# Two attentions and a gate on one core: five score products and six maxima tasks issued in another order

## The chip, the core and the metric

The kernel runs on one core of one Trainium2 chip. A core has a matrix engine (PE, whose weight loads the profile lists apart as PEld), a vector engine (DVE), a scalar engine (ACT), a general engine (POOL) and SyncE (SP), which here only starts transfers. Each engine runs its own instructions in the order in which the program issued them; semaphores tie the engines together. Matrix products land in PSUM, eight banks of 512 fp32 columns for each of 128 partitions. The metric is the device time of one execution in microseconds (us), and of several runs the median.

## The reference: what is computed

Input x has 2048 rows of 512 columns; there are 32 heads of 16 columns. Two attention blocks read the same x, and a gate mixes them:

```
g = sigmoid((x * gate_w).sum(-1))
a: q, k, v = x @ wq, x @ wk, x @ wv; 4 segments of 512 rows:
   p = softmax(q k^T / 4 + causal mask), within the segment
   o = sigmoid(beta) * (phi(q) M) / (phi(q) z + 1e-6) + (1 - sigmoid(beta)) * (p v)
   then M += phi(k)^T v, z += sum phi(k);  phi(t) = t + 1 if t > 0 else exp(t)
   a = o @ A_wo
b: q, k, v = x @ wqkv; p = softmax(q k^T / 4) over all 2048 rows; b = (p v) @ B_wo
out = g * a + (1 - g) * b
```

A is causal within a segment of 512 rows and carries a memory from segment to segment; B is full attention over 2048 rows.

## The kernel before, in words

**Units.** The work is cut into 64 units, each of four heads and 512 queries: units 0 to 31 belong to A, units 32 to 63 to B. After a stage of projections (up to about 400 us of the profile), the main loop runs 32 steps. Step k computes unit 32 + k of B and unit k of A, and beside them the row maxima that the softmax of the next units needs.

**Positions.** A step has NG = 37 positions n. At positions 0 to 31 stand the 32 groups of score products of B, and at 32 to 36 the five groups of A (`GA`). A position issues, in this order: `t_group` (the transposed score products of two heads, L537, and two exponentials on ACT, L543, that write the weights to `raw`); the work that `plan` and `extras` hold for the position; and `pvs`, products with the values into the bank `pvb` (L559). In A, POOL then clears the part above the diagonal (L546). The tasks of `plan` at a position of B go inside `t_group`, between its first and its second product (`mid`).

**Maxima tasks.** `s_b` (L467) and `s_a` (L442) make score products again, untransposed, into one of the two double banks `sbk`, and DVE reduces each to its row maxima (L476 for B; L460 or L462 for A). The two double banks are taken in turn, so a task waits until DVE has read the task two before it. Positions 0 to 31 have one `s_b` task each. Positions 32 to 36 have the six `s_a` tasks in the order of `ST_A` (L700): one at 32, one at 33, two at 34, one at 35, one at 36. A task (i, p) of A handles row block i, 128 queries that see 128 * (i + 1) keys: (3, p) has 512 columns in each of two products, (2, p) has 384; (1, None) does both pairs p with 256 columns each, and (0, None) both with 128. Each pair p adds four small mask products (L456). Longer rows cost DVE more.

**Halves of the array.** Scores contract over 64 rows, so a product uses the upper or the lower half of the array (j = 0 or 1), and products of different halves run side by side. Products with the values use all 128 rows.

**The output projection.** From step 9 to step 30, position 1 also holds `out_rows` (L639): 24 products in 12 pairs (upper half, lower half) of the weights `wh`, `wl` with the rows `oh`, `ol` (L644), accumulating in one misc bank and one half of an `sbk`. Steps alternate between a = 0 and a = 1, the two input halves; a = 1 adds up and stores. After its third pair, out_rows issues the tasks handed to it as `inner`: in these steps the one `s_b` task that `plan` holds for position 1. `split` work for the next rows (`oh` on ACT, `ol` on POOL, L622) stands at the end of every even step.

**Banks.** `t_group`, `out_rows` and `m_rows` draw from the three banks T3 = tb0, tb1, mb; `bank` (L88) hands out the one that was taken longest ago. A group that takes a bank waits until ACT has read it.

**The A order elsewhere.** The first six tasks of A (unit 0) are taken in the same order from a list that is issued in pairs inside the projection stage (L764, L783).

Of the kernel before, what the change touches and what calls it, by code (L numbers as in the profile page):

```python
# [23 lines left out]
NT = SEQ // 128  # L24
# [10 lines left out]
def gated_mix_kernel(ctx, tc, xt, wq, wk, wv, wo, beta, wqkv, wob, gate_w, out):  # L35
# [49 lines left out]
    SBK = [PS.tile([128, 2, C], FT, name=f"sbk{i}") for i in range(2)]  # L85
    lru = []

    def bank(allowed):  # L88
        b = min(allowed, key=lambda a: max([n for n, x in enumerate(lru) if x is a], default=-1))
        lru[:] = [x for x in lru if x is not b] + [b]  # L90
        return b
# [3 lines left out]
    def misc():  # L95
        return bank(mode["misc"])
# [12 lines left out]
    def rot(key, lst):  # L109
        i = cnt.get(key, 0)  # L110
        cnt[key] = i + 1
        return lst[i % len(lst)]
# [287 lines left out]
    def q_of(u):  # L400
        return QA[u % 2] if u < 32 else QB[u % 3]

    def k_of(u, p):
        return KA[u % 2][:, p] if u < 32 else KB[(u - 32) % 3][:, p]
# [113 lines left out]
    AT = {}  # L518
# [3 lines left out]
    def t_group(u, n, banks, between=()):  # L522


        kd, qd, c = UN[u]
        bs = [bank(banks) for _ in range(2)]
        c0 = 0
        for it, hs in (((n // 2, (n % 2 * 2, n % 2 * 2 + 1)),) if kd == "B" else GA[n]):
            q0 = 128 * it if kd == "A" else 0
            w = C - q0  # L530
            pn = it if kd == "B" else it % 2
            for j, h in enumerate(hs):
                if j:
                    for f in between:
                        f()
                r = slice(64 * j, 64 * j + 64)
                nc.tensor.matmul(bs[j][:, c0:c0 + w], k_of(u, h // 2)[r, 128 * it:128 * it + 128],  # L537
                                 q_of(u)[r, h // 2, q0:], start=True, stop=True)
                PT[u, it, h] = PTILE[pn % 2][:, 2 + j if (kd, it) == ("A", 2) else h][:, c0:c0 + w]
            c0 += w  # L540
        for j in range(2):
            pt = PTILE[pn % 2][:, 2 + j if (kd, n) == ("A", 4) else hs[j]]
            nc.scalar.activation(pt, bs[j], AF.Exp, scale=SCALE)  # L543
            if kd == "A":
                m = pt[:, :128] if n < 2 else pt.rearrange("p (a t) -> p a t", a=4)[:, ::3 if n < 4 else 2]
                nc.gpsimd.affine_select(out=m, in_=m, pattern=[[1, 128]] if n < 2 else [[0, 2], [1, 128]],  # L546
                                        compare_op=OP.is_ge, fill=0.0, base=0, channel_multiplier=-1)
# [89 lines left out]
            nc.sync.dma_start(outr[tt * 128:(tt + 1) * 128, :], AT["yo"])  # L637

    def out_rows(c, t, a, inner):  # L639
        b = [misc(), rot("s", SBK)[:, 0]]  # L640
        for n, (oi, wi, g) in enumerate([(oi, wi, g) for oi, wi in TERMS for g in range(4)]):
            for j in range(2):
                r = slice(64 * j, 64 * j + 64)
                nc.tensor.matmul(b[j], (AT["oh"], AT["ol"])[oi][r, g, a], (AT["wh"], AT["wl"])[wi][r, g, a],  # L644
                                 start=n == 0, stop=n == 11)
            if n == 2:
                for f in inner:
                    f()
                rot("s", SBK)
        if a == 0:  # L650
            AT["y"] = [AT["L"].tile([128, DM], FT, name=n) for n in ("yo", "yp")]
            nc.scalar.activation(AT["y"][0], b[0], AF.Copy)
            nc.vector.tensor_copy(AT["y"][1], b[1])
        else:
            tt = 4 * c + t
            y0, y1 = AT["y"]
            y2 = AT["L"].tile([128, DM], FT, name="yq")
            nc.scalar.activation(y2, b[0], AF.Copy)
            nc.vector.tensor_tensor(y1, b[1], y1, op=OP.add)
            nc.gpsimd.tensor_tensor(y0, y0, y2, op=OP.add)  # L660
            nc.gpsimd.tensor_tensor(y0, y0, y1, op=OP.add)
            nc.sync.dma_start(outr[tt * 128:(tt + 1) * 128, :], y0)
# [33 lines left out]
    def todo(fn, *a):  # L696
        return lambda: fn(*a)

    ST_B = [(i, p, kc) for i in range(4) for p in range(2) for kc in range(4)]
    ST_A = [(3, 0), (3, 1), (2, 0), (2, 1), (1, None), (0, None)]  # L700

    def s_tasks(u):
        return [todo(s_a, u, *t) for t in ST_A] if u < 32 else [todo(s_b, u, *t) for t in ST_B]

# [83 lines left out]
    for blk in range(16):  # L788
        g, c = divmod(blk, 4)
        pg, pc = divmod(blk - 1, 4)  # L790
        if blk == 4:
            mode["misc"] = TB + [MB, PVB]
        rate = len(ST_A + ST_B) / SPILLS if 4 <= blk < 14 else 0
        if blk == 14:
# [3 lines left out]
        n = blk + 1 + (c == 2)  # L798
# [74 lines left out]
    def late():  # L873
        proj.close()
        L = AT["L"] = ctx.enter_context(tc.tile_pool(name="late", bufs=1))
        VB[1] = L.tile([128, NT, 8, E + 1], FT, name="vb1")
        AT["o"] = [L.tile([128, 4, 2, C], FT, name=f"o{n}") for n in range(2)]
        AT["wh"] = L.tile([128, 4, 2, DM], FR, name="wh")
        AT["wl"] = L.tile([128, 4, 2, DM], FR, name="wl")
        AT["d"] = [L.tile([128, C], FT, name=f"d{n}") for n in range(2)]  # L880
        AT["oh"] = L.tile([128, 4, 2, 128], FR, name="oh")
        AT["ol"] = L.tile([128, 4, 2, 128], FR, name="ol")
        for p in range(2):
            set_aux(KB[2][:, p], 0)

    T3 = TB + [MB]
# [4 lines left out]
    def pvs(k, n):  # L891

        ua, ub = k, 32 + k
        if n == 0:
            if k:
                pv(ua - 1, 2)
                fin_copy(ua - 1)
        elif k == 31 and n < 2 * NT:
            if n % 2 and n > 1:
                pv(ub, n // 2 - 1)  # L900
        elif 2 <= n < 2 * NT + 2:
            pv(ub, n // 2 - 1, n % 2 * 256, n % 2 * 256 + 256)
            if n == 2 * NT + 1:
                fin_copy(ub)
        elif n > 2 * NT + 1:
            m = n - 2 * NT - 2
            if m < 2:
                pv(ua, 0, 256 * m, 256 * m + 256)
            else:
                pv(ua, 1)  # L910
                pv(ua, 3)

    def extras(k):

        pre, post = {}, {}
        if not k:
            for n in range(4):
                pre[2 * n] = [fill[n - 4]]
        post[2 * S_LAST + 4] = [todo(m_rows, k + 1)]
        for n, at in [(k - 9, 1)] + [(23, 2 * OMI)] * (k == 31):  # L920
            if n >= 0:
                rows = (n // 8, n // 2 % 4, n % 2)
                pre[at] = [todo(out_rows, *rows, plan.pop((k, at))) if k < 31 else todo(out_mm, *rows)]
        return pre, post

    def beside(k, it):
# [28 lines left out]
    plan = {}  # L955

    def spread(tasks, gs):
        for n, p in enumerate(gs):
            plan.setdefault(p, []).extend(tasks[len(tasks) * n // len(gs):len(tasks) * (n + 1) // len(gs)])

    for k in range(31):
# [3 lines left out]
        else:  # L965
            spread(st33[EARLY:], sorted([(0, n) for n in range(2 * S_LAST)] + [(0, 2 * n) for n in range(4)]))
        for n, t in enumerate(ST_A):
            plan.setdefault((k, 2 * NT + n - (n > 2)), []).append(todo(s_a, k + 1, *t))

    ex = [extras(k) for k in range(32)]  # L970
    for k in range(32):
        ua, ub = k, 32 + k
        banks = T3 + [b[:, 0] for b in SBK] * (k == 31)
        for n in range(NG):
            it = n // 2 if n < NG - 1 else NT + 2
            mid = plan.pop((k, n)) if n < 2 * NT and (k, n) in plan else []
            t_group(*(ub, n) if n < 2 * NT else (ua, n - 2 * NT), banks, mid)
            for f in plan.get((k, n), []) + ex[k][0].get(n, []):
                f()
            pvs(k, n)  # L980
            for f in ex[k][1].get(n, []):
                f()
            if n % 2 == 0 and n < NG - 1:
                continue
            beside(k, it)
            if it == S_LAST:
                m_chain(k + 1)
            if it == 4 and not k:
                late()
            if it == 4 and not k:  # L990
                load_q(ub + 2)
                for c in range(NC4):
                    load_kb(2, c)
            if it == NT and k < 29:
                load_q(ub + 3)
                load_kb(k + 3)
            if it == 6 and k < 31:
                load_q(ua + 1)
                load_ka(ua + 1)
                if (ua + 1) % 2 == 0:  # L1000
                    load_va(ua + 1)
            if it == 9:
                if k % 2 == 0 and k < 30:
                    load_vb(k // 2 + 1)
                if 1 <= k <= 4:
                    load_wo(k - 1)
# [55 lines left out]
```

## Time and profile before

| | |
|---|---|
| median of 3 runs | 1941.73 us (1938.82 to 1942.05) |
| the profiled execution's own time | 1942.89 us |
| its span in the profile | 1941.2 us |
| granted PE clock | 0.998 of full speed |
| busy: PE, DVE, ACT, POOL | 1915.3, 1622.4, 1438.0, 345.1 us |
| DMA | 222.54 MB, 115 GB/s over the span |

The profiled execution took 1.16 us more than the median of the runs. Lines of a timeline give the start, the length, the engine, the source line, the operation, `output<-inputs` by the names of the program, the shape, the count of merged instructions, and in brackets how long the engine had been idle and who ended that. PE's records overlap, since two halves of the array and successive products run into each other; the distance between starts says more than the length of one. Lines of the stretches give a window, its length, and for each engine busy time and count of instructions.

### The profile page before, as it was taken

How to read it: one execution, taken by the hardware profiler on the slowest of the kernel's cores; microseconds unless marked ns; L12 is line 12 of the kernel's file. 1: busy time of each engine (PE TensorE's matmuls, PEld its weight loads, DVE VectorE, ACT ScalarE, POOL GpSimd, SP SyncE). 2: the span in 40 equal slices, each digit the busy share in tenths (PEclk: the TensorE clock that was granted, in tenths of full speed). 3: DMA queues.
4: the chain of work that ended last, by engine and by line, in shares of the span. 5: the costliest groups of instructions: out<-in, count | busy, mean ns of one | idle time of the engine just before them, and what ended most of it. 6: DMA issues, size and time to landing. Idle time of an engine off the chain costs nothing.

```text
span 1941.2 us, 44264 instructions
## 1 busy us (share of the span) xinstructions
PE 1915.3 (99%) x17749; PEld 933.8 (48%) x17749; DVE 1622.4 (84%) x1689; ACT 1438.0 (74%) x2710; POOL 345.1 (18%) x687
## 2 busy tenths in 40 slices
PE   7999998999999999999999999999999999999999
PEld 5887776444444444444444444444444444444445
DVE  6135765799999999999999999999999999999942
ACT  4233332688888888888888888888888888888894
POOL 5200000011211111112121212121212121212122
PEclk9999999999999999999999999999999999999999
DMA  7666556655543444444434344444444444434111
GB/s 218 167 208 189 183 186 180 162 118 115 100 116 88 106 90 105 88 115 86 115 88 115 88 115 88 109 95 109 95 101 99 95 104 92 107 90 107 50 49 59
DMA packets 163794, 222.54 MB, mean 115 GB/s; under 512 B 39916, under 2 KB 90556, under 8 KB 157828
## 3 DMA queue, kind: packets, MB, share of 16 engines
q1 hardware_dynamic: 159284, 211.41, 44.0%
q0 software_dynamic: 3248, 8.03, 2.2%
q8 instruction: 140, 2.29, 0.5%
q14 instruction: 66, 0.54, 0.1%
q10 hardware_dynamic: 1056, 0.26, 0.1%
HBM read 147.95 MB, written 68.16 MB: 111 GB/s over the span
## 4 chain that ended last, share of the span: by engine, by line
PE 95%; DVE 2%; DMA 1%; SPq 1%; ACT 0%; issue 0%; DVEq 0%; ACTq 0%
PE pvb L559 34%; PE tb L537 18%; PE sbk L474 12%; PE mb L537 9%; PE tb L304 4%; PE sbk L452 3%; PE tb L644 2%; PE mb L304 2%; PE sbk L287 1%; PE tb L287 1%; PE sbk L456 1%; PE mb L644 1%; PE pvb L304 1%; PE mb L287 1%; PE pvb L287 1%; DMA dA<-st 1%
## 5 line engine op out<-in xcount | busy, mean ns | idle before, releaser
L476 DVE TENSOR_REDUCE mxb<-sbk 128x2 f32<-128x1024 f32 x1024 | 1228.7, 1221 | 52.1 <-PE tb L537 24.0
L543 ACT ACTIVATE raw<-tb 128x512 f32<-128x512 f32 x1555 | 887.1, 598 | 125.7 <-PE tb L537 82.2
L559 PE MATMUL pvb<-raw,vb 128*17 128x256 f32 (+1 forms) x8072 | 639.8, 388 | 0.0
L543 ACT ACTIVATE raw<-mb 128x512 f32<-128x512 f32 x782 | 467.8, 598 | 60.3 <-PE mb L537 34.0
L474 PE MATMUL sbk<-xh,qb 64*128 64x512 f32 x1344 | 473.3, 442 | 4.8 <-DMA xh<-dB 3.4
L537 PE MATMUL tb<-qb,xh 64*128 64x512 f32 x872 | 351.2, 444 | 0.0
L559 PEld LDWEIGHTS pvb<-raw,vb 128*17 128x17 f32 x8072 | 134.9, 95 | 338.8 <-issue 333.4
L474 PE MATMUL sbk<-kb,qb 64*128 64x512 f32 x704 | 239.0, 442 | 0.0
L537 PEld LDWEIGHTS tb<-qb,xh 64*128 64x128 f32 x872 | 146.0, 184 | 174.4 <-issue 86.6
L537 PE MATMUL mb<-qb,xh 64*128 64x512 f32 x445 | 198.1, 445 | 0.0
L474 PEld LDWEIGHTS sbk<-xh,qb 64*128 64x128 f32 x1344 | 191.9, 184 | 11.6 <-DVE mxb L476 5.6
L537 PE MATMUL tb<-qb,kb 64*128 64x512 f32 x470 | 189.9, 444 | 0.8 <-DVE st L314 0.8
L546 POOL TENSOR_SCALAR_AFFINE_SELECT raw<-raw 128x256 f32<-128x256 f32 (+1 forms) x320 | 115.5, 361 | 354.2 <-ACT raw L543 346.3
L460 DVE TENSOR_REDUCE mx<-sbk 128x2 f32<-128x768 f32 (+1 forms) x128 | 136.7, 1090 | 23.2 <-POOL o L608 13.7
L537 PEld LDWEIGHTS mb<-qb,xh 64*128 64x128 f32 x445 | 82.0, 184 | 92.7 <-issue 47.9
L537 PEld LDWEIGHTS tb<-qb,kb 64*128 64x128 f32 x470 | 79.7, 184 | 96.1 <-issue 49.8
L537 PE MATMUL mb<-qb,kb 64*128 64x512 f32 x234 | 104.8, 448 | 0.0
L474 PEld LDWEIGHTS sbk<-kb,qb 64*128 64x128 f32 x704 | 96.7, 184 | 5.8 <-issue 3.2
L559 PE MATMUL pvb<-raw,va 128*17 128x256 f32 (+2 forms) x1280 | 94.8, 384 | 0.8 <-ACT pvs L568 0.8
L452 PE MATMUL sbk<-ka,qa 64*128 64x256 f32 (+3 forms) x512 | 87.8, 358 | 1.1
L311 ACT ACTIVATE st<-tb 128x512 fp32r<-128x512 f32 x33 | 19.8, 599 | 81.9 <-DVE phi L310 46.2
L603 POOL TENSOR_TENSOR o<-o,d 128x512 f32<-128x512 f32 x31 | 39.7, 1281 | 227.2 <-DMA d<-rd 177.1
(315 smaller groups left out, 2036.6 us busy)
## 6 DMA issues: line engine op xcount, KB each, us to landing
xh<-dB SPq DMA_DIRECT2D x38, 512.0 KB
vb<-vdB SPq DMA_DIRECT2D x16, 1088.0 KB
dB<-st SPq DMA_DIRECT2D x64, 256.0 KB
dA<-st SPq DMA_DIRECT2D x64, 256.0 KB
pd<-pvs SPq DMA_DIRECT2D x64, 256.0 KB
kb<-dB SPq DMA_DIRECT2D x22, 512.0 KB
xh<-dB SPq DMA_DIRECT2D x38, 256.0 KB
qb<-dB SPq DMA_DIRECT2D x64, 128.0 KB
```

What stands on the lines that cost most here:

```text
L287: nc.tensor.matmul(b, lhs, WV[wi][:, k, :], start=n == 0, stop=n == 11)
L304: nc.tensor.matmul(b, WS[ws][w][wi][:, k, :], (XH, XL)[xi][c][:, k, :], start=n == 0, stop=n == 11)
L452: nc.tensor.matmul(b[:, j, c0:c0 + n], q_of(u)[r, p, i * 128:(i + 1) * 128], k_of(u, p)[r, :n], start=True, stop=False)
L460: nc.vector.tensor_reduce(m[:, :, p, i], b[:, :, :n], axis=AX.X, op=OP.max)
L474: nc.tensor.matmul(b[:, j], q_of(u)[r, p, i * 128:(i + 1) * 128], k_of(u, p)[r, kc * C:(kc + 1) * C], start=True, stop=True)
L476: nc.vector.tensor_reduce(MXB[u][:, :, p, i, kc], b, axis=AX.X, op=OP.max)
L537: nc.tensor.matmul(bs[j][:, c0:c0 + w], k_of(u, h // 2)[r, 128 * it:128 * it + 128], q_of(u)[r, h // 2, q0:], start=True, stop=True)
L543: nc.scalar.activation(pt, bs[j], AF.Exp, scale=SCALE)
L546: nc.gpsimd.affine_select(out=m, in_=m, pattern=[[1, 128]] if n < 2 else [[0, 2], [1, 128]], compare_op=OP.is_ge, fill=0.0, base=0, channe ...
L559: nc.tensor.matmul(PVB[32 * h:32 * h + E + 1, q0 + lo:q0 + hi], vt[:, it, 4 * q + h, :], pt[:, lo:hi], start=it == 0 and lo == 0, stop=it ...
L603: nc.gpsimd.tensor_tensor(o, o, d, op=OP.mult)
L644: nc.tensor.matmul(b[j], (AT["oh"], AT["ol"])[oi][r, g, a], (AT["wh"], AT["wl"])[wi][r, g, a], start=n == 0, stop=n == 11)
```

## The change

Three edits.

1. In steps 9 to 30 the second group of B (position 1) is no longer issued ahead of the output projection. It becomes the `inner` work of `out_rows`: after the third pair, `t_group` issues its first product, then the `s_b` task of position 1, then its second product and two exponentials; then pairs four to twelve follow.
2. The projection's misc bank is remembered as `AT["ob"]`, and the third group (position 2) of these steps takes its two banks from T3 without that one.
3. `ST_A` goes from row blocks 3, 3, 2, 2, 1, 0 to 0, 2, 2, 3, 3, 1. The places stay: one task at positions 32 and 33, two at 34, one at 35 and at 36.

The line that defines `banks` moves into the inner loop, without further effect.

```
     def out_rows(c, t, a, inner):
-        b = [misc(), rot("s", SBK)[:, 0]]
+        AT["ob"] = misc()
+        b = [AT["ob"], rot("s", SBK)[:, 0]]
...
-    ST_A = [(3, 0), (3, 1), (2, 0), (2, 1), (1, None), (0, None)]
+    ST_A = [(0, None), (2, 0), (2, 1), (3, 0), (3, 1), (1, None)]
...
-                pre[at] = [todo(out_rows, *rows, plan.pop((k, at))) if k < 31 else todo(out_mm, *rows)]
+                pre[at] = [todo(out_rows, *rows, [todo(t_group, 32 + k, at, T3, plan.pop((k, at)))]) if k < 31 else
+                           todo(out_mm, *rows)]
...
-        banks = T3 + [b[:, 0] for b in SBK] * (k == 31)
         for n in range(NG):
+            banks = T3 + [b[:, 0] for b in SBK] * (k == 31)
             it = n // 2 if n < NG - 1 else NT + 2
             mid = plan.pop((k, n)) if n < 2 * NT and (k, n) in plan else []
-            t_group(*(ub, n) if n < 2 * NT else (ua, n - 2 * NT), banks, mid)
+            if 9 <= k < 31 and n == 2:
+                banks = [b for b in T3 if b is not AT["ob"]]
+            if not (9 <= k < 31 and n == 1):
+                t_group(*(ub, n) if n < 2 * NT else (ua, n - 2 * NT), banks, mid)
```

## The prediction, made before the changed kernel was run

> **What bounds the kernel now.** I read the page first: shares of busy time and the chain that ended last.
>
> ```profile
> span 1941.2 us, 44264 instructions
> PE 1915.3 (99%) x17749; PEld 933.8 (48%) x17749; DVE 1622.4 (84%) x1689; ACT 1438.0 (74%) x2710; POOL 345.1 (18%) x687
> ...
> PE 95%; DVE 2%; DMA 1%; SPq 1%; ACT 0%; issue 0%; DVEq 0%; ACTq 0%
> ```
>
> PE is busy 99% of the span and carries 95% of the chain, so time is won only where PE stands still or refills. A busy PE record hides short stalls, since records overlap; so I went on to the timeline of one step and to the distances between starts. First the five A positions of a step (here 1222.19 to 1229.97), as stretches: one line for each position 32 to 36, then the parts from the first maxima product to the first value product of positions 32, 33, 35 and 36, then positions 1 and 2 together, including the projection, in a step with a = 1 and in one with a = 0.
>
> ```profile
> 1222.19:1223.57 1.38, 1.38 (x21) 0.82 (x18) 1.15 (x2) 1.30 (x3) 0.17 (x1) 1.00 0.00 0
> 1223.57:1224.86 1.29, 1.29 (x20) 0.54 (x17) 1.28 (x2) 0.94 (x3) 0.44 (x3) 1.00 0.00 0
> 1224.86:1226.70 1.84, 1.80 (x29) 1.02 (x25) 1.77 (x3) 1.84 (x4) 0.96 (x3) 1.00 0.03 13
> 1226.70:1228.20 1.50, 1.50 (x28) 0.95 (x25) 1.28 (x2) 0.93 (x3) 0.66 (x3) 1.00 0.77 220
> 1228.20:1229.97 1.77, 1.77 (x36) 1.10 (x32) 1.48 (x2) 1.26 (x3) 1.00 (x4) 1.00 0.74 216
> 1222.54:1223.01 0.47, 0.47 (x8) 0.34 (x7) 0.42 (x1) 0.39 (x2) 0.00 (x0) 1.00 0.00 0
> 1223.91:1224.30 0.39, 0.39 (x8) 0.11 (x4) 0.39 (x1) 0.14 (x1) 0.26 (x1) 1.00 0.00 0
> 1227.03:1227.64 0.61, 0.61 (x16) 0.49 (x12) 0.51 (x1) 0.35 (x1) 0.16 (x1) 1.00 0.67 225
> 1228.54:1228.98 0.44, 0.44 (x16) 0.39 (x12) 0.44 (x1) 0.18 (x1) 0.31 (x1) 1.00 0.58 177
> 1231.19:1235.87 4.68, 4.68 (x45) 3.05 (x41) 3.48 (x5) 2.40 (x5) 0.24 (x1) 1.00 0.95 160
> 1181.75:1186.65 4.90, 4.90 (x45) 3.38 (x41) 3.43 (x5) 2.62 (x6) 2.12 (x1) 1.00 0.95 134
> ...
> 1180.34 1.06 ACT L622 ACTIVATE oh<-o 128x1024 fp32r<-128x1024 f32 x1
> ```
>
> The first number after the window is its length. The five positions take 1.38, 1.29, 1.84, 1.50 and 1.77, together 7.78 us. Position 34 stands out. Its rows, and those of position 35, which also issues two tasks' worth of products:
>
> ```profile
> 1223.19 4.35 DVE L460 TENSOR_REDUCE mx<-sbk 128x2 f32<-128x1024 f32 x4 [0.23 <-PE sbk L456]
> 1225.20 0.39 PE L452 MATMUL sbk<-ka,qa 64*128 64x384 f32 x2
> 1225.43 0.23 PE L456 MATMUL sbk<-cmask,crows 64*128 64x64 bf16 x4
> 1225.70 0.19 PEld L452 LDWEIGHTS sbk<-ka,qa 64*128 64x128 f32 x2 [0.15 <-DVE mx L460]
> 1225.98 0.23 PE L456 MATMUL sbk<-cmask,crows 64*128 64x64 bf16 x4
> 1226.14 0.62 PE L559 MATMUL pvb<-raw,va 128*17 128x256 f32 x8
> ...
> 1227.03 0.33 PE L452 MATMUL sbk<-ka,qa 64*128 64x256 f32 x2
> 1227.21 0.23 PE L456 MATMUL sbk<-cmask,crows 64*128 64x64 bf16 x4
> 1227.28 0.36 PE L452 MATMUL sbk<-ka,qa 64*128 64x256 f32 x2
> 1227.48 0.23 PE L456 MATMUL sbk<-cmask,crows 64*128 64x64 bf16 x4
> 1227.64 0.63 PE L559 MATMUL pvb<-raw,va 128*17 128x256 f32 x8
> ```
>
> At 1225.70 the weight load of position 34's second task waits for DVE: task four may write its double bank only when DVE has reduced task two, and DVE works through four reductions in one piece (4.35 us). At position 35 nothing waits, and product, masks, product, masks follow at 0.18, 0.07, 0.20 and 0.16. DVE's view by source line says how long a reduction is and how often this wait occurs:
>
> ```profile
> L460 DVE TENSOR_REDUCE mx<-sbk x128: 947/1088/1228, 289.1 to 1866.7; 128x2 f32<-128x1024 f32 x64, 128x2 f32<-128x768 f32 x64
>   PEld sbk L452: 4.7, 30
> ```
>
> 947 ns is a row block 2, 1228 ns a row block 3; the wait is there in 30 steps, so it belongs to the order. Then positions 0 to 3 of the step with a = 1, and how often the projection's products wait for ACT:
>
> ```profile
> 1229.97 0.49 PE L537 MATMUL mb<-qb,kb 64*128 64x512 f32 x1
> 1230.74 1.23 DVE L476 TENSOR_REDUCE mxb<-sbk 128x2 f32<-128x1024 f32 x1 [0.95 <-PE tb L537]
> 1230.99 0.59 ACT L543 ACTIVATE raw<-tb 128x512 f32<-128x512 f32 x1
> 1231.19 0.49 PE L537 MATMUL tb<-qb,kb 64*128 64x512 f32 x1
> 1231.64 0.18 PEld L644 LDWEIGHTS tb<-wh,oh 64*128 64x128 f32 x1 [0.26 <-ACT raw L543]
> 1231.97 0.39 PE L644 MATMUL tb<-wh,oh 64*128 64x512 f32 x1
> 1232.44 0.39 PE L474 MATMUL sbk<-xh,qb 64*128 64x512 f32 x2
> 1234.75 0.40 PE L537 MATMUL tb<-qb,kb 64*128 64x512 f32 x1
> 1235.87 0.50 PE L537 MATMUL tb<-qb,kb 64*128 64x512 f32 x1
> ...
>   ACT raw L543: 6.2, 22
> ```
>
> The second group starts at 1231.19, the projection at 1231.64. It takes the bank that the first group filled second; ACT empties it until 1231.58, so its weights load only then. 22 waits are 22 steps. Free-running pairs follow each other at 0.232 (1231.97 to 1234.75 are 12 pairs); the first pair after value products or after a wait takes 0.34 (1231.64 to 1231.97), so 0.11 is the price of weights that were not loaded ahead.
>
> **The change part by part.** No instruction is added or removed on PE, DVE, ACT or POOL, and no transfer moves on SP's or POOL's queue; only orders and banks change.
>
> *Order of the maxima tasks.* A position is scores, task(s), value products: 0.34 (1224.86 to 1225.20), the task part, then 0.56 (1226.14 to 1226.70), or at position 36 0.99 (1228.98 to 1229.97). Task parts by the stretches: row block 3 takes 0.39 (at 33) or 0.47 as the first of the stage (at 32), blocks 1 and 0 0.61 and 0.44. A product 128 columns narrower saves a quarter of a pair, 0.06, so block 2 alone is 0.33. The new positions:
> - 32, block 0: 1.38 - 0.39 + 0.44 = 1.43; the 0.08 of the first task stays.
> - 33, block 2: 1.29 - 0.06 = 1.23.
> - 34, blocks 2 and 3: first product 0.23 (1225.20 to 1225.43), masks 0.07, second product 0.20 as at 35 plus 0.11 for 256 columns more, masks 0.16: 0.77 and, with 0.34 and 0.56, 1.67. The second task now needs the reduction of position 33. That task starts at 1222.19 + 1.43 + 0.34 = 1223.96; DVE starts 0.18 after its part ends (1223.01 to 1223.19 now), so at 1224.47, and ends 0.95 later at 1225.42. PE wants the bank at 1224.85 + 0.34 + 0.30 = 1225.49. That nearly meets; I add 0.03: 1.70.
> - 35, block 3: 1.50 - 0.61 + 0.39 = 1.28.
> - 36, block 1: 1.77 - 0.44 + 0.61 = 1.94.
>
> The sum is 7.58 against 7.78: 0.20 for each of the 31 stages with such tasks (steps 0 to 30), 6.2 us. What can be late next: position 35 shrinks from 1.50 to 1.28, and the scores of 36 need ACT to have emptied a bank of 35, so part of the gain may be lost there; the lower end is no gain, the upper 0.30, the whole stall (0.94 from 1225.20 to 1226.14 less 0.23 + 0.07 + 0.26 + 0.16) and the 0.08 at 32. I take 0.20, since its terms are all rows. In the projection stage the six tasks of unit 0 go in pairs with a double bank each; both orders leave a pair nothing to wait for, so it costs nothing.
>
> *The second group inside the projection.* The projection now takes the bank that the first group left alone, and the stall at 1231.64 goes. Counted from 1231.19 there are 14 pairs as before: 12 of the projection and two mixed ones (score product beside maxima product, twice). Halves alternate throughout. That is 0.34 + 13 x 0.232 = 3.35, then position 2 as now, 1.12 (1234.75 to 1235.87): 4.47. The banks of the second group are those of the first, whose second exponential ends at 1231.58 or so; its first product is wanted three pairs later, at 1231.19 + 0.34 + 2 x 0.232 = 1232.00. That is covered by the three pairs. Position 2 reuses both banks 2.3 us after its first use, where two exponentials of 0.59 fit.
>
> A new wait stands in their place. The maxima task of position 1 writes the double bank of position 0, which DVE reduces from 1230.74 to 1231.97. Now PE wants it at 1232.44 (by 0.23 ahead for its weights); afterwards at 1232.00. Behind it on PE stand the second score product and nine pairs. The nearest rows are those of step 7, which has no projection, so that position 2 comes this early:
>
> ```profile
> 692.76 0.38 PE L537 MATMUL mb<-qb,xh 64*128 64x512 f32 x1
> 693.25 0.19 PEld L474 LDWEIGHTS sbk<-xh,qb 64*128 64x128 f32 x2 [0.19 <-DVE mxb L476]
> ```
>
> There the half was free 0.23 after 692.76, at 692.99, and the load came at 693.25, which with 0.11 of loading costs 0.37. That is the upper bound of the new wait; the lower is 0. Here the bank comes at 1231.97 + 0.05 = 1232.02 (the lag by position 34: two reductions of 1.228 from 1223.19 end at 1225.65, the load follows at 1225.70), so the half loses 0.02 and 0.11, some 0.13 to 0.15: I take 0.15, as the row 1231.64 to 1231.97 shows a full 0.11 after a wait. Positions 1 and 2 then take 4.62 in place of 4.68 (a = 1, 11 steps) and 4.90 (a = 0, 11 steps; ACT is later there, as it first splits rows for 1.06 us at 1180.34, and the stall is longer). The gain is 11 x 0.06 + 11 x 0.28 = 3.7 us, with bounds of 11 x 0.21 + 11 x 0.43 = 7.0 (no wait) and -11 x 0.16 + 11 x 0.06 = -1.1 (wait of 0.37).
>
> The Trainium skill speaks on this wait ("TensorE: Matmul & The Clock Gate", Part 1, on engine queue depths): PE can pull weight loads ahead of matmuls in flight. By it the 0.11 would be hidden and the gain would be 22 x 0.11 = 2.4 us larger; here the row at 1225.70 shows a load that waits for its bank held back with its matmul.
>
> Sum: 6.2 + 3.7 = 9.9 us off the profiled 1942.89, 1933.0; the median of the runs lies 1.16 below that execution, so 1931.8.
>
> **Rivals.**
> - *Slower: the maxima chain of A runs into the projection.* The last task of a step becomes block 1 (1.23 us on DVE) in place of block 0. If DVE is then still reducing when position 0's maxima are ready, the reduction now at 1230.74 starts late, the task inside the projection waits for it, and PE with it. For: this wait is new and has PE's whole queue behind it. Against: the new stage also starts DVE earlier; with the new positions, position 34's first reduction starts near 1225.6, and 0.95 + 3 x 1.23 later, at 1230.2, DVE is free; position 0 starts at 1229.77 and needs it 0.77 on (1229.97 to 1230.74), at 1230.54. Price: 22 us for each us of delay, while 9.9 is gained; over 0.2% slower from (9.9 + 3.9) / 22 = 0.63 of delay. One block-1 reduction late (1.0 beyond the margin) gives 1942.89 - 9.9 + 22 - 1.16 = 1953.8.
> - *The new wait takes what the stall gave.* It costs 0.37 in each step: +1.1, with 6.2 from the order alone: 1936.6. For: step 7's row. Against: there DVE freed the bank later.
> - *No gain from the order*, because ACT's banks at 34 and 36 or POOL's masks become the next to end: 3.7 alone, 1938.0. For: positions of 1.23 and 1.28 against two exponentials of 0.59. Against: these waits price at 0.11 or less each.
> - *Nothing waits.* No loss inside the projection (7.0) and 6.2 from the order: 1928.5. The skill's rule of loads pulled ahead would lead near it.
>
> **How the numbers follow.** Chances: my forecast 48%, the wait eats the stall 15%, no gain from the order 12%, nothing waits 15%, slower 6%, no effect at all 4%. Runs spread by 0.17% (1938.82 to 1942.05), so 0.2%, 3.9 us, is about what can be told from no change: faster means under 1937.85. Forecast, nothing waits, the second rival and half of the third lie there: 0.84; the other half and no effect make 0.10; slower 0.06. The range takes in these cases but the last two: 1926 (bounds 31 x 0.30 = 9.3 and 7.0 together give 1925.4) to 1939.
>
> **What would show it.** In the changed profile: the wait of the maxima products for DVE (30 times now) gone or under 0.05 each; five A positions at 7.6 together; the 22 waits of the projection for ACT gone; a weight load of the maxima product inside the projection waiting for DVE about 0.1 to 0.2 in 22 steps; positions 1 and 2 at 4.6 in both kinds of steps. The prediction is wrong if the reduction of position 0 starts later than 0.77 after its scores, or if PE waits for ACT at 34 or 36.

## The result

| | before | changed |
|---|---|---|
| median | 1939.82 us (9 runs) | 1946.28 us (9 runs) |
| ratio | | 1.003, 95% interval 1.0016 to 1.0043 |
| profiled execution's span | 1941.2 us | 1947.7 us |

The change made the kernel 6.5 us slower, where 9.9 faster was forecast. The page of the changed kernel hardly looks different: the same count of instructions on PE, PE busy 0.6 us longer, and PE's share of the longer span 98% where it was 99%.

```profile
span 1947.7 us, 44246 instructions
PE 1915.9 (98%) x17749; PEld 940.3 (48%) x17749; DVE 1620.5 (83%) x1689; ACT 1443.1 (74%) x2710; POOL 345.1 (18%) x687
...
PE 96%; DVE 2%; ACT 1%; SPq 1%; DMA 1%; issue 0%; POOL 0%; DVEq 0%; ACTq 0%
```

The stretches tell where the time went. Each line is a window of the span, its length, and the busy time of PE, PEld, DVE, ACT and POOL, then the granted clock and what the DMA engines did. First the kernel before, from A of step 0 to A of step 30, from there to A of step 31, and to the end:

```profile
397.74:1862.08 1464.34, 1463.24 (x15269) 616.47 (x15265) 1368.23 (x1303) 1240.40 (x2313) 268.90 (x555) 1.00 0.44 99
1862.08:1906.50 44.42, 44.35 (x336) 18.51 (x333) 17.41 (x31) 38.67 (x79) 9.38 (x16) 1.00 0.11 34
1906.50:1941.20 34.70, 29.91 (x172) 20.91 (x168) 10.24 (x26) 9.80 (x22) 8.90 (x19) 1.00 0.21 70
```

The same three stretches of the changed kernel:

```profile
396.22:1851.34 1455.12, 1454.01 (x15269) 619.25 (x15265) 1366.90 (x1303) 1242.22 (x2313) 268.76 (x554) 1.00 0.44 100
1851.34:1912.29 60.95, 51.93 (x338) 20.10 (x334) 16.82 (x31) 42.57 (x80) 9.48 (x17) 1.00 0.08 25
1912.29:1947.70 35.41, 30.79 (x172) 21.21 (x168) 10.25 (x26) 9.34 (x20) 8.90 (x19) 0.98 0.20 68
```

Thirty steps are shorter by 9.2 us (1464.34 to 1455.12), nearly what the prediction had for them. One stretch, from A of step 30 to A of step 31, in which B of the last step is computed, went from 44.42 to 60.95: 16.5 us lost in a place that the prediction did not look at. PE's busy time there is 51.93 of 60.95, so PE stands still for 9 us, and it is busy 7.6 longer with the same products, which overlap less; ACT's busy time grew by 4 us only. With 1.5 less ahead of the loop and 0.7 more in the tail the sum is +6.5. The 1.5 is no effect of its own that these profiles could show: that stretch takes 391.30 to 397.74 in them, and 395.52 in a run below that issues there just what the kernel before does. The 0.7 comes back with the runs below.

**The last step.** Two positions of B in step 31 before, in the timeline:

```profile
1880.26 0.49 PE L537 MATMUL tb<-qb,xh 64*128 64x512 f32 x2
1880.60 0.39 PE L537 MATMUL mb<-qb,xh 64*128 64x512 f32 x1
1880.77 0.50 PE L537 MATMUL sbk<-qb,xh 64*128 64x512 f32 x1
...
1882.22 0.49 PE L537 MATMUL sbk<-qb,xh 64*128 64x512 f32 x1
```

Four score products go to tb, tb, mb and sbk; five banks take turns, and the next four begin 1.96 us later (1880.26 to 1882.22). Changed:

```profile
1870.53 0.50 PE L537 MATMUL sbk<-qb,xh 64*128 64x512 f32 x2
1871.06 2.27 ACT L543 ACTIVATE raw<-sbk 128x512 f32<-128x512 f32 x4 [0.81 <-PE sbk L537]
1871.71 0.18 PEld L537 LDWEIGHTS sbk<-qb,xh 64*128 64x128 f32 x1 [0.99 <-ACT raw L543]
1873.60 0.50 PE L537 MATMUL sbk<-qb,xh 64*128 64x512 f32 x2
```

All four go to sbk. The load for the third ends an idle time of 0.99, when ACT has emptied the bank of the first, and the pattern takes 3.07 us (1870.53 to 1873.60). The waits of the window 1851.34 to 1912.29, with total, count and longest, say the same. In the same stretch of the kernel before, the waits of `sbk L537` for ACT come to 0.9 us in 4; here to:

```profile
PEld sbk L537 <- ACT raw L543: 31.0, 45, 1.1
```

**Why.** The bank chooser remembers what it handed out by object, not by memory:

```
    def bank(allowed):
        b = min(allowed, key=lambda a: max([n for n, x in enumerate(lru) if x is a], default=-1))
        lru[:] = [x for x in lru if x is not b] + [b]
        return b
```

In step 31 the list holds two slices, `b[:, 0]` of the two sbk, and a slice is a new object each time it is written. Before, the list was made once per step, and its five objects lasted for the step. The change makes it once per position: the new slices are in no memory of the chooser, rank as longest unused, and win at every position. Two banks remain where there were five. The section on the change calls the moved line "without further effect"; that was wrong. The list also serves the A positions of step 31, which lie in the tail: there, too, the score products of the changed kernel all go to sbk.

**The thirty steps.** The five A positions of a step in the changed kernel:

```profile
1216.21:1217.63 1.42, 1.42 (x26) 0.95 (x22) 1.14 (x2) 1.34 (x3) 0.22 (x1) 1.00 0.00 0
1217.63:1218.87 1.24, 1.24 (x21) 0.55 (x17) 0.76 (x2) 0.84 (x3) 0.37 (x2) 1.00 0.05 13
1218.87:1220.55 1.68, 1.68 (x29) 0.97 (x26) 1.34 (x2) 1.68 (x4) 0.78 (x3) 1.00 0.00 0
1220.55:1221.90 1.35, 1.35 (x24) 0.73 (x20) 1.35 (x3) 0.99 (x3) 0.72 (x3) 1.00 0.87 243
1221.90:1223.78 1.88, 1.88 (x36) 1.13 (x32) 1.88 (x2) 1.42 (x3) 1.27 (x4) 1.00 0.71 146
```

Their sum is 7.57 (forecast 7.58, before 7.78), and no weight load of a maxima product of A waits for DVE any more. Then positions 0 to 2 with the projection, and the rows around the new wait:

```profile
1223.78:1229.59 5.81, 5.81 (x56) 4.08 (x52) 4.32 (x6) 3.22 (x7) 0.63 (x2) 1.00 1.02 160
1224.55 1.23 DVE L476 TENSOR_REDUCE mxb<-sbk 128x2 f32<-128x1024 f32 x1 [0.42 <-PE tb L537]
1225.57 0.18 PEld L537 LDWEIGHTS mb<-qb,kb 64*128 64x128 f32 x1
1225.80 0.39 PE L537 MATMUL mb<-qb,kb 64*128 64x512 f32 x1
1225.83 0.19 PEld L474 LDWEIGHTS sbk<-xh,qb 64*128 64x128 f32 x2
```

5.81 in place of 5.90 (1229.97 to 1235.87 before) in a step with a = 1; over all 22 steps the means are 5.80 now, and 5.90 (a = 1) and 6.12 (a = 0) before. DVE ends the reduction of position 0 at 1225.78, and the weights of the maxima product load at 1225.83, at the time at which their product should already run: the first score product had its weights 0.23 ahead (1225.57 for 1225.80). From there the lower half runs some 0.13 behind the upper until the value products.

One thing more belongs to the single execution: early in the loop a maxima product waits once for DVE, for 1.43 us. Five of the eight runs below have a wait of this kind in the first three steps, at changing places, of 0.8 to 1.5 us; it blurs sums over the loop, so single positions are the better measure.

```profile
435.05 0.19 PEld L474 LDWEIGHTS sbk<-kb,qb 64*128 64x128 f32 x2 [1.43 <-DVE mxb L476]
```

### The profile page after: what moved, and what is told of

It is laid out like the page before. It is cut to its first block, busy times and chain, and to the rows that moved or that the text cites. A ratio compares the mean times of both kernels' runs of the same rounds, so it can differ in the third digit from the quotient of the medians.

```text
span 1947.7 us, 44246 instructions
## 1 busy us (share of the span) xinstructions
PE 1915.9 (98%) x17749; PEld 940.3 (48%) x17749; DVE 1620.5 (83%) x1689; ACT 1443.1 (74%) x2710; POOL 345.1 (18%) x687
## 4 chain that ended last, share of the span: by engine, by line
PE 96%; DVE 2%; ACT 1%; SPq 1%; DMA 1%; issue 0%; POOL 0%; DVEq 0%; ACTq 0%
PE pvb L559 33%; PE tb L537 17%; PE sbk L474 12%; PE mb L537 9%; PE tb L304 5%; PE sbk L452 3%; PE mb L304 2%; PE pvb L304 1%; PE sbk L287 1%; PE tb L287 1%; PE tb L645 1%; PE sbk L645 1%; PE sbk L537 1%; PE sbk L456 1%; PE mb L287 1%; PE pvb L287 1%
## 5 line engine op out<-in xcount | busy, mean ns | idle before, releaser
L543 ACT ACTIVATE raw<-tb 128x512 f32<-128x512 f32 x1525 | 869.0, 596 | 130.5 <-PE tb L537 92.7
L543 ACT ACTIVATE raw<-mb 128x512 f32<-128x512 f32 x769 | 458.2, 596 | 65.7 <-PE mb L537 42.3
L537 PE MATMUL tb<-qb,xh 64*128 64x512 f32 x861 | 347.4, 441 | 0.0
L537 PEld LDWEIGHTS tb<-qb,xh 64*128 64x128 f32 x861 | 145.1, 184 | 165.4 <-issue 81.7
L537 PE MATMUL tb<-qb,kb 64*128 64x512 f32 x454 | 185.7, 444 | 0.8 <-DVE st L314 0.8
L537 PE MATMUL mb<-qb,xh 64*128 64x512 f32 x419 | 186.2, 444 | 0.0
L460 DVE TENSOR_REDUCE mx<-sbk 128x2 f32<-128x1024 f32 (+1 forms) x128 | 133.9, 1088 | 25.9 <-PE sbk L456 25.9
L537 PEld LDWEIGHTS tb<-qb,kb 64*128 64x128 f32 x454 | 76.7, 184 | 92.3 <-ACT raw L543 45.1
L537 PEld LDWEIGHTS mb<-qb,xh 64*128 64x128 f32 x419 | 77.3, 184 | 85.7 <-ACT raw L543 42.6
L537 PE MATMUL mb<-qb,kb 64*128 64x512 f32 x250 | 110.5, 442 | 0.0
L452 PE MATMUL sbk<-ka,qa 64*128 64x512 f32 (+3 forms) x512 | 84.4, 355 | 0.0
L462 DVE TENSOR_REDUCE mx<-sbk 128x4 f32<-128x512 f32 x64 | 61.4, 959 | 21.9 <-PE sbk L456 21.9
```

What stands on the lines that cost most here:

```text
L452: nc.tensor.matmul(b[:, j, c0:c0 + n], q_of(u)[r, p, i * 128:(i + 1) * 128], k_of(u, p)[r, :n], start=True, stop=False)
L460: nc.vector.tensor_reduce(m[:, :, p, i], b[:, :, :n], axis=AX.X, op=OP.max)
L462: nc.vector.tensor_reduce(m[:, :, :, i], b.rearrange("q j (p k) -> q j p k", p=2)[:, :, :, :n], axis=AX.X, op=OP.max)
```

## The experiments

**Theory:** the edits of the order and of the projection gain about 10 us in the thirty steps, as reckoned, and the list that is made anew at each position costs the last step 16.5. **Rival:** the new orders leave the last step in a bad state (of banks, DVE or transfers), and the moved line is innocent.

### The list made once per step

```
-        for n in range(NG):
-            banks = T3 + [b[:, 0] for b in SBK] * (k == 31)
+        once = T3 + [b[:, 0] for b in SBK] * (k == 31)
+        for n in range(NG):
+            banks = once
```

This is the changed kernel otherwise.

> The changed kernel, but the list of banks is built once per step, as before the change. Theory (the two maxima edits gain 10.8 us up to the start of A in step 30, and the rebuilt list alone costs the last step 16.5 us, because the bank chooser compares objects by identity and no longer recognises the two sbk halves it has just handed out): about 10 us faster than the kernel before, near 1929; the distance from the start of A in step 30 to the start of A in step 31 is back from 60.95 to about 44.4, and the waits of score products into sbk for ACT (34.0 us, 52) nearly vanish. Rival (the new order of maxima or the new use of banks in step 30 leaves the last step in a bad state): that distance stays above 55 and the time stays near 1946.

Measured: 1929.24 us against 1940.23 of the kernel before, ratio 0.9944 (0.9932 to 0.9957). The stretches, from A of step 0 to A of step 30, to A of step 31, to the end, and positions 0 to 2 of one step:

```profile
394.29:1848.30 1454.01, 1453.86 (x15268) 619.31 (x15264) 1365.66 (x1303) 1242.82 (x2313) 268.54 (x554) 1.00 0.44 100
1848.30:1892.73 44.43, 44.40 (x337) 18.64 (x333) 16.77 (x31) 38.79 (x79) 9.62 (x17) 1.00 0.11 34
1892.73:1927.41 34.68, 29.91 (x172) 20.91 (x168) 10.25 (x26) 9.80 (x22) 8.90 (x19) 1.00 0.21 70
1220.69:1226.50 5.81, 5.81 (x57) 4.08 (x54) 4.32 (x6) 3.23 (x7) 0.65 (x2) 1.00 1.06 167
```

The last step is back at 44.43, the tail at 34.68, and the thirty steps keep their gain: 10.3 us (1464.34 less 1454.01). The rival falls.

### The moved line alone

```
-        banks = T3 + [b[:, 0] for b in SBK] * (k == 31)
         for n in range(NG):
+            banks = T3 + [b[:, 0] for b in SBK] * (k == 31)
```

> The kernel before, with the one line that makes the list of banks moved into the loop over positions, nothing else. Theory of the rebuilt list: 16 to 17 us slower than before, near 1956; step 31 at about 61 from A to A, all other steps unchanged at 49.45 and 49.2. Rival (that line is without effect, as the front text says): same as before, 1940.

Measured: 1957.92 us, ratio 1.0093 (1.0075 to 1.0111).

```profile
395.52:1859.81 1464.29, 1463.22 (x15268) 616.71 (x15264) 1368.17 (x1303) 1239.68 (x2313) 268.79 (x555) 1.00 0.44 99
1859.81:1921.09 61.28, 51.88 (x337) 20.07 (x333) 17.38 (x31) 42.58 (x80) 9.39 (x16) 1.00 0.08 25
1921.09:1956.60 35.51, 30.88 (x172) 21.17 (x168) 10.24 (x26) 9.34 (x20) 8.90 (x19) 1.00 0.21 68
```

The thirty steps are those of before (1464.29 and 1464.34), the last step takes 61.28 and the tail 35.51, 16.9 and 0.8 more than before. One line that computes nothing costs 17 to 18 us (17.7 by the medians).

### Two banks and no others

In the changed kernel with the list made once per step, step 31 gets the two sbk halves alone:

```
+        once = T3 if k < 31 else [b[:, 0] for b in SBK]
```

> The changed kernel, but in step 31 the list holds only the two sbk halves, built once per step. Theory of identity (the rebuilt list makes the chooser hand out the two sbk halves at every position, and two banks cannot cover two exponentials): this is the changed kernel again, about 3.08 us for two positions in the last step, 61 from A to A, 1946. Rival (something else in the rebuilt list, as a longer search or other waits, costs the time): the last step clearly below 61.

Measured, one run: 1944.38 us, where the kernel before took 1939.01 beside it, and the same last step as in the changed kernel:

```profile
1846.36:1907.30 60.94, 51.95 (x337) 20.10 (x333) 16.73 (x31) 42.60 (x80) 9.35 (x16) 1.00 0.08 25
```

60.94 against 60.95, and 35.40 in the tail against 35.41: that the chooser hands out two banks is the whole loss; nothing else in the new list costs time.

### The order alone

The kernel before with the new `ST_A`.

> The kernel before with the new order of the maxima tasks alone. Theory: the five A positions sum to 7.57 in place of 7.78 in each of 31 stages, so 6 to 7 us faster, near 1933.5; step lengths 49.24 (a = 0) and 48.99 (a = 1), the 30 waits of maxima products for DVE gone. Rival (the gain in the steps comes from the projection edit): steps at 49.45 and 49.2, time within 2 us of before.

Measured: 1932.06 us, ratio 0.9959 (0.9944 to 0.9973). From A of step 0 to A of step 30, and positions 1 and 2 of a step with a = 0:

```profile
391.61:1849.04 1457.43, 1456.73 (x15268) 611.03 (x15264) 1364.62 (x1303) 1240.12 (x2313) 268.63 (x554) 1.00 0.45 100
1172.03:1176.78 4.75, 4.75 (x44) 3.11 (x40) 3.41 (x5) 2.50 (x6) 1.99 (x1) 1.00 1.00 164
```

6.9 us less than before in this window, where 30 stages x 0.21 make 6.3. In the 11 steps with a = 0 positions 1 and 2 together gain 0.13 as well (4.75 to 4.78 in place of 4.90), which was not expected; single waits early in the loop take about 1 us back. The medians show 8.2, 1.3 more than this window; most of the rest would lie ahead of the loop, where the profiles spread too far to tell (391.30 to 396.63 in the seven with a new order, 394.79 to 397.74 in the three with the old one). For the 0.13, a reading that the rows allow, but that was not tested by itself: ACT's split of the rows, which stands at the end of even steps, starts further ahead of position 0, and so ACT comes to the exponentials of position 0 sooner, whose banks the second group waits for. In this run and before:

```profile
1170.49 1.06 ACT L622 ACTIVATE oh<-o 128x1024 fp32r<-128x1024 f32 x1
1170.81 0.50 PE L537 MATMUL tb<-qb,xh 64*128 64x512 f32 x1
1171.44 0.60 ACT L543 ACTIVATE raw<-tb 128x512 f32<-128x512 f32 x1
```

```profile
1180.54 0.50 PE L537 MATMUL tb<-qb,xh 64*128 64x512 f32 x1
1181.28 0.60 ACT L543 ACTIVATE raw<-tb 128x512 f32<-128x512 f32 x1
```

The split starts 0.32 ahead of the scores here, 0.20 before (1180.34 to 1180.54), and the first exponential 0.63 after them here, 0.74 before.

### The second group inside the projection alone

The changed kernel with the list made once per step and the old `ST_A`.

> The second group inside the projection alone: old order of maxima, list of banks built once per step. Theory: positions 0 to 2 from 5.90 and 6.12 to 5.80, so 0.1 and 0.3 in 11 steps each, 4 to 5 us faster, near 1935.5; the 22 waits of the projection for ACT gone. Rival (the old order keeps DVE later and the task inside the projection waits longer than 0.13): gain under 2 us.

Measured: 1937.55 us over 10 runs, ratio 0.9984 (0.9974 to 0.9993): 2.7 us against the 4 to 5 expected.

```profile
394.79:1856.18 1461.39, 1459.87 (x15268) 624.50 (x15264) 1369.62 (x1303) 1242.25 (x2313) 268.71 (x555) 1.00 0.44 99
```

Over this window the gain is 3.0 us. Means of the position lengths of all steps put positions 0 to 2 at 0.32 (a = 0) and 0.09 (a = 1) less, as expected, 4.5 us in 22 steps, while a single wait early in the loop gives back 0.8 and the other positions of B are some 0.002 longer each, about 1 us in all; the granted clock of this profile is 0.997 where that of before is 0.998. So the edit is worth 4.5 by its place, and the runs show 2.7 with an interval of about 1 to 5 us; why the other positions are longer was not looked into.

### The same group one pair later and one pair sooner

In `out_rows`, with the list made once per step:

```
-            if n == 2:
+            if n == 3:
```

> The changed kernel with the list of banks built once per step, and the second group issued after the fourth pair of the projection in place of the third. Theory (inside the projection the maxima task waits some 0.13 us for the reduction of position 0, and the halves of the array stay that far apart until the value products): one pair later the bank is free, so positions 0 to 2 take 5.68 in place of 5.80, 22 steps x 0.12 = 2.6 us off the run with the third pair, near 1926.6. Rival (the 0.12 are the price of mixing the tasks, not of the wait): positions 0 to 2 stay at 5.80, 1929.

Measured: 1928.21 us, ratio 0.9939 (0.9926 to 0.9953) to 1939.01 of the kernel before, against 0.9944 for the third pair; the medians differ by 1.0 where 2.6 was expected, and these runs cannot tell that from nothing. The place shows it: positions 0 to 2, and the products where the group begins.

```profile
1217.40:1223.08 5.68, 5.68 (x56) 3.50 (x52) 4.28 (x6) 3.08 (x6) 0.51 (x2) 1.00 1.01 154
1219.44 0.40 PEld L474 LDWEIGHTS sbk<-xh,qb 64*128 64x128 f32 x2
1219.66 0.39 PE L537 MATMUL mb<-qb,kb 64*128 64x512 f32 x1
1219.66 0.61 PE L474 MATMUL sbk<-xh,qb 64*128 64x512 f32 x2
```

5.68, as expected: the maxima product has its weights 0.22 ahead and starts with the score product. And after the second pair (`n == 1`):

> The same with the second group after the second pair. Theory of the wait: it comes 0.23 sooner and so waits 0.23 longer, positions 0 to 2 at about 6.03, 22 x 0.23 = 5 us more than with the third pair, near 1934. Rival (price of mixing): 5.80 and 1929.

```profile
1225.16:1231.19 6.03, 6.03 (x57) 3.59 (x53) 4.32 (x6) 3.42 (x7) 0.73 (x2) 1.00 1.03 167
1226.96 0.38 PE L537 MATMUL mb<-qb,kb 64*128 64x512 f32 x1
1227.21 0.18 PEld L474 LDWEIGHTS sbk<-xh,qb 64*128 64x128 f32 x2 [0.30 <-DVE mxb L476]
1227.21 0.50 PE L474 MATMUL sbk<-xh,qb 64*128 64x512 f32 x2
```

6.03, as expected, and 1936.9 us in one run, where about 1934 was expected. One pair sooner costs 0.22, nearly the full 0.23 between two pairs, and one pair later saves 0.13: the price is the wait for DVE, not the mixing. The Trainium skill ("TensorE: Matmul & The Clock Gate", Part 1, on engine queue depths) says that PE can pull weight loads ahead of matmuls in flight. These runs agree where the bank is free (0.22 ahead) and show its limit: a load that waits for its bank goes no sooner than its product (1227.21).

### Another order: 0, 1, 2, 2, 3, 3

```
+    ST_A = [(0, None), (1, None), (2, 0), (2, 1), (3, 0), (3, 1)]
```

with the list made once per step.

> The changed kernel with the list of banks built once per step, and the row blocks in the order 0, 1, 2, 2, 3, 3. Theory (position 34's second task needs the reduction of position 33 to be done): block 1 at position 33 takes DVE 1.23 and ends later, so the wait of the maxima product for DVE comes back with about 0.2 to 0.3 in each of 31 stages, and the five A positions sum to 7.75 to 7.85 in place of 7.57, 6 to 8 us more, near 1936. Rival (what helps is only that a small block stands first): sum near 7.57, 1929.

Measured, one run: 1940.08 us, where about 1936 was expected. Positions 33 and 34, all five, and how often the maxima products of A wait for DVE:

```profile
1221.13:1222.59 1.46, 1.46 (x26) 0.78 (x22) 0.75 (x2) 1.05 (x3) 0.56 (x3) 1.00 0.05 11
1222.59:1224.44 1.85, 1.81 (x30) 1.02 (x26) 1.79 (x3) 1.72 (x4) 0.88 (x4) 1.00 0.12 46
1219.70:1227.61 7.91, 7.87 (x116) 4.66 (x112) 6.71 (x7) 6.30 (x12) 3.29 (x10) 1.00 0.34 86
  DVE mx L462: 4.7, 30
```

The wait is back, 30 times, at position 34, and the sum is 7.91, even above the 7.75 to 7.85 expected. A small block at the head does not help by itself. The second task of position 34 waits for the reduction of position 33, which in this order is that of block 1 (1.23 us) and not of block 2 (0.95).

## Why the prediction was wrong

Point by point, by its own steps:

- **What bounds the kernel, and the stall at position 34:** right. It went with the order and came back with another order.
- **The order of the maxima tasks, 0.20 in each of 31 stages, 6.2 us:** right; 0.21 in the changed kernel, and PE is held by ACT neither at 34 nor at 36 (the loads ahead of their scores come after the same idle time of 0.42, whether ACT is named for it or not). Position 35 took 1.35 where 1.28 was forecast, and position 36 1.88 where 1.94 was; the sum holds. The effect on positions 1 and 2 with a = 0, 0.13 in 11 steps, was missed.
- **The second group inside the projection, positions 1 and 2 at 4.62 (with position 0: 5.84), 3.7 us:** right in mechanism and near in size: 5.81, since the wait costs 0.13 and not 0.15. Alone it gains 4.5 by its place; on top of the order 3.1 is left to gain, as the order already takes 0.13 of the stall with a = 0. By place the two edits gain 6.5 + 1.4 + 3.1 = 11.0 together; that is also what the medians show with the list made once per step (1940.23 to 1929.24), though the window of thirty steps shows 10.3.
- **"No instruction is added or removed ...; only orders and banks change":** here the prediction failed. The sentence is true of the count of instructions, but the prediction then priced banks only at positions 1 and 2 of steps 9 to 30, where the diff names them, and gave the moved line no price and no place. It changes which banks step 31 gets, and costs 16.5 us there: more than both gains together. The sum needs it as a third term: -6.2 - 3.7 + 16.5 = +6.6, and the measured medians differ by +6.5. So close a sum is in part luck: the tail adds 0.7 to the loss, and the gains were 11.0 and not 9.9.
- **The rivals:** the slower one was the maxima chain of A running into the projection, and it did not happen: DVE still starts the reduction of position 0 at 0.77 after its scores (1223.78 to 1224.55). None of the rivals was about the last step. The range, 1926 to 1939, holds both versions with the list made once per step (1929.24 and 1928.21), and not the change as it was made.

## What to carry to other kernels

Where a program that writes the instructions keeps state by object (a chooser of banks, a cache of tiles), a line moved into a loop can change the instructions without changing a value: price each moved line by what the generator does with it, and compare which bank or buffer each product names in the two programs ahead of any reckoning of time. A gain in 30 equal steps can be lost in the one step that is different; read the odd step's rows too. A product that is put between others should stand where its bank comes free before its weights are to load: here one pair later took the whole wait of 0.13 away, and one pair sooner added 0.22.

The version with the list made once per step and the second group after the fourth pair beats both kernels: 1928.21 us, 0.9939 of the kernel before. Its lead over the third pair shows in the positions, not in the medians.

## What the runs showed of the hardware

In these runs a wait of one half of the array is not made up. In the projection of the changed kernel one half starts late once, by 0.13, and after nine more pairs the first products of position 2 are still that far apart:

```profile
1228.35 0.40 PE L537 MATMUL mb<-qb,kb 64*128 64x512 f32 x1
1228.48 0.49 PE L474 MATMUL sbk<-xh,qb 64*128 64x512 f32 x2
```

The products with the values, which use both halves, end it: after them the halves begin together again (1229.59 and 1229.60). A stall hardly shows in PE's busy time: position 34 before shows PE busy 1.80 of 1.84 us, and without the stall it takes 1.68, though one of its two tasks is then a longer one.
